# A new order of work in the attention part of a fused attention and feed-forward kernel: sync queue, weight operations, score thirds and key products

## The chip, the core and the metric

The kernel runs on one core of a Trainium2 chip. Its engines are TensorE (PE, with its weight loads shown as PEld), VectorE (DVE), ScalarE (ACT), GpSimd (POOL) and SyncE (SP), which here only issues DMAs. Each engine works through its own list of instructions in order, and they meet at semaphores. The metric is the device time of one execution in microseconds.

## What is computed

The first part is attention over 8 batches, 12 heads, 448 positions and a head size of 64, with scores capped by a tanh. Its output, put back to 8 x 448 x 768, goes through a feed-forward layer that mixes each position with the one before it.

```
scores = cap * tanh(scale * q @ k.T / cap)
attn = exp(scores - max) / (sum + 1e-9)
x = attn @ v                                   # -> (8, 448, 768)
xk = mu_k * x + (1 - mu_k) * x_prev            # x_prev: one position earlier
xr = mu_r * x + (1 - mu_r) * x_prev
k = relu(xk @ w_k)                             # 768 -> 1024
out = sigmoid(xr @ w_r) * ((k * k) @ w_v)
```

The weights come as 64-bit floats and are turned into 32-bit ones by the kernel itself.

## The kernel before

**Steps.** The 96 heads are taken as 48 pairs. The first part of the kernel is a loop of 54 steps (`NSTEP`), one for each pair and six that drain it. What one step emits is written out as a list of words; `step` reads it from left to right, and so each engine's order is the order of the words. There are four lists: `START_EVEN` and `START_ODD` for the steps below `SW` (14), `EVEN` and `ODD` for the rest. Step i works on several pairs at once:

- `S0`, `S1`, `S2` (L216): scores of pair i, one third of the keys each, into a PSUM tile `s`, of which there are two, taken in turn. `L` (L227), in even steps, is the leftover 64 keys of pairs i and i+1, done in quadrants of the array. For pairs below 14 (`RAW`) the scores multiply the loaded floats themselves; later pairs use a high and a low part that POOL makes two steps ahead (`qk_high`, `qk_low`).
- `tanh`, `exp` (L237, L243) on ACT; `red` (L273) on DVE sums the exponentials.
- `V` (L252): values of pair i-1, into a PSUM tile `pv`, of which there are two. `VL` (L262) adds the leftover keys of pairs i-2 and i-1, in quadrants too.
- `gather` (L282): four small DMAs that bring the sums of pair i-1 together, `recip` (L286, DVE) inverts them, `rec_store` (L294) and `rec_load` (L297) send the result through DRAM and back as a broadcast.
- `norm` (L303, DVE), `mix_old` (L306, ACT), `mix_new` (L316, DVE), `x_high`, `x_low` (L322, L325, POOL), `x_store` (L331): pair i-2 is normalised, mixed and split. `mix_old` overwrites the `pv` tile, and `mix_new` is the last to read it, so it is `mix_new` of pair i-2 that frees the tile for `V` two pairs on.
- `K` (L342): some of the 1152 matmuls of `xk @ w_k`, 18 to a PSUM tile `kps`, of which there are two. `KE` and `KO` tell how many each of the four `K` words of an even and an odd step makes: 28 in an even step, 20 in an odd one, from step 7 on (`KFIRST`). `relu` (L360, ACT) and `k_store` (L367, a DMA issued by ACT) take out every tile finished so far.
- `weight_load` (L374) brings one of 44 weight pieces; `more` brings a second one in the steps that `MORE` names. `weight_abs` (L392, ACT) and five operations `f` (L415 to L423, DVE; `weight_rest` does all that are left) convert it, `weight_sum` (L428, POOL) and, for `w_k`, `weight_low` (L441, DVE) finish it, `weight_store` (L447) sends the pieces of `w_r` and `w_v` to DRAM.

**Queues.** All loads and stores but `k_store` are issued by SP, in the order of the words, so an issue that waits for a semaphore holds up every later one. `gather` waits for the last `red` of the step before, `rec_store` for `recip`, `rec_load` for the landing of `rec_store`.

**The second part** (L660 on) runs 28 chunks of 128 positions through `w_r` and `w_v`. Nothing in it is changed.

Of the kernel before, what the change touches and what calls it, by code (L numbers as in the profile page):

```python
# [38 lines left out]
QA = QM + KL  # L39
NSTEP = NPAIR + 6  # L40
RAW = 14
SW = 14
MORE = (1, 7, 8, 9, 10)
KFIRST = 28
KE, KO, KT = (7, 7, 7, 7), (5, 5, 5, 5), 8
HALF = (slice(0, 64), slice(64, 128))
NB = 2 * S // 32

# [2 lines left out]

START_EVEN = """gather weight_load load_v load_vl more load_qk weight_low S0 S1 K V VL L weight_rest f norm f tanh0 exp0
qk_high weight_sum tanh1 exp1 relu k_store f recip red0 qk_low tanhL K S2 mix_old mix_new x_high x_low red1
tanh2 relu expL redL exp2 k_store K K red2 f f weight_abs relu k_store rec_store rec_load x_store
weight_store"""
START_ODD = """gather more load_qk load_v weight_load f f f S0 S1 V S2 f f weight_low K tanh0 relu exp0 norm red0
weight_rest weight_sum tanh1 recip rec_store qk_high tanh2 mix_old mix_new x_high qk_low x_low k_store exp2 K
red2 relu exp1 red1 k_store K K relu weight_abs k_store weight_store x_store rec_load"""  # L60
EVEN = """weight_load gather load_vl load_v load_qk weight_rest weight_low f S0 S1 V VL L S2 f f tanh1 tanh0 exp1 exp0
qk_high weight_sum norm recip x_store more K qk_low tanhL relu mix_old red1 mix_new x_high x_low k_store K
expL relu tanh2 redL f f red0 exp2 red2 k_store K K relu k_store weight_abs rec_store rec_load weight_store"""
ODD = """gather more weight_store load_v weight_load f weight_rest S0 S1 V S2 weight_low f K relu tanh0 k_store exp0
red0 qk_high weight_sum tanh1 f norm f recip load_qk rec_store K exp1 red1 f tanh2 mix_old mix_new x_high
qk_low x_low exp2 relu k_store weight_abs K K relu k_store red2 rec_load x_store"""


def f(ap):
# [3 lines left out]
class Body:  # L73
# [446 lines left out]
    def step(self, i):  # L520
# [9 lines left out]
        nk = 0  # L530
        for op in ((START_EVEN if even else START_ODD) if i < SW else EVEN if even else ODD).split():
            g = ()
# [12 lines left out]
            elif op == "more":  # L545
                for _ in range(MORE.count(i)):
                    self.weight_load()
# [170 lines left out]
```

## Time and profile before

| | |
|---|---|
| median of the runs | 983.07 us |
| lowest of the runs | 980.41 us |
| the profiled execution | 981.96 us |
| its span, first to last instruction | 979.8 us |
| PE busy in the span | 937.7 us |
| DVE busy | 652.7 us |
| ACT busy | 478.1 us |
| POOL busy | 255.4 us |

The busy time of PE is that of overlapping matmuls with modelled ends, so an engine shown busy can still lose some tenths of a microsecond at each wait. In the rows below, an arrow `<-` behind a time in brackets names what ended an engine's idle time, by tile and line; SPq and ACTq are DMA issues. Where an engine waits for several semaphores, the one that came last is named.

### The profile page before, as it was taken

What the parts mean: (1) busy time and instruction counts of PE and PEld (TensorE: products, weight loads), DVE (VectorE), ACT (ScalarE), POOL (GpSimd) and SP (SyncE); (2) the same over time, 40 slices, a digit from 0 to 9 for tenths busy, and PEclk for the clock granted to TensorE, in tenths of its full rate; (3) what the DMA queues carried; (4) which work ended last, traced back from release to release, by engine and by line L of the source; (5) the groups of instructions that cost most, each with busy time, mean ns of one, the idle gap of its engine ahead of it and who ended that gap; (6) DMA issues with size and microseconds to landing.
All of it is one profiled execution on the core that took longest, in us unless ns stands there. A gap on an engine that the chain in (4) does not pass through costs nothing.

```text
span 979.8 us, 14498 instructions
## 1 busy us (share of the span) xinstructions
PE 937.7 (96%) x5244; PEld 737.8 (75%) x5244; DVE 652.7 (67%) x1126; ACT 478.1 (49%) x578; POOL 255.4 (26%) x289
## 2 busy tenths in 40 slices
PE   5878999999999999999999999999999999999997
PEld 1225556656666656666667889999999999999997
DVE  5889998798878888885554685554564464464460
ACT  6877787768777877777774112221221221221220
POOL 1434445455555555545431210000000000000000
PEclk9789999999999999999999999999999999999999
DMA  5455555665656656665534843332332332233220
GB/s 163 144 171 179 192 180 188 178 213 182 202 173 193 207 177 188 193 191 157 167 109 131 265 141 88 105 108 67 96 109 71 91 108 78 84 108 86 78 70 35
DMA packets 124704, 138.85 MB, mean 142 GB/s; under 512 B 19664, under 2 KB 109776, under 8 KB 124624
## 3 DMA queue, kind: packets, MB, share of 16 engines
q1 hardware_dynamic: 115408, 123.16, 41.6%
q10 hardware_dynamic: 9216, 14.68, 4.0%
q8 instruction: 43, 0.70, 0.3%
q14 instruction: 37, 0.30, 0.1%
HBM read 92.64 MB, written 42.40 MB: 138 GB/s over the span
## 4 chain that ended last, share of the span: by engine, by line
PE 52%; DVE 21%; DMA 17%; SPq 5%; ACT 3%; issue 2%; POOL 0%; DVEq 0%; ACTq 0%; POOLq 0%
PE pvv L500 23%; PE pr L500 17%; DVE r L275 7%; DMA sq<-r 6%; PE kps L356 5%; SPq L284 4%; PE pv L259 3%; DMA rec_d<-rs 3%; DVE wt L415 3%; DMA r<-rec_d 2%; PE s L224 2%; DVE sr L288 2%; DVE wa L417 2%; DVE xk L319 1%; DMA w<-wr 1%
## 5 line engine op out<-in xcount | busy, mean ns | idle before, releaser
L91 ACT CAST xh<-t 128x768 fp32r<-128x768 f32 x27 | 22.6, 838 | 308.7 <-DVE t L483 308.7
L275 DVE TRANSPOSE_TENSOR_REDUCE r<-p 128x28 f32<-128x896 f32 x144 | 153.4, 1076 | 13.4 <-ACT p L250 13.1
L240 ACT ACTIVATE p<-s,scl_t 128x896 f32<-128x896 f32 x144 | 141.1, 995 | 17.6 <-PE s L224 14.6
L250 ACT ACTIVATE p<-p,cap_t 128x896 f32<-128x896 f32 x144 | 147.3, 1039 | 2.4
L515 DVE TENSOR_TENSOR o<-pvv,rsg 128x768 f32<-128x768 f32 (+1 forms) x29 | 27.0, 930 | 181.2 <-PE pvv L500 180.3
L356 PE MATMUL kps<-xkh,wkh 128*128 128x448 f32 x384 | 143.8, 374 | 2.8 <-ACT ko L363 2.6
L259 PE MATMUL pv<-p,rv 128*64 128x448 f32 x576 | 127.2, 579 | 20.0 <-DMA rv<-v 13.2
L356 PE MATMUL kps<-xkl,wkh 128*128 128x448 f32 x384 | 142.7, 371 | 0.0
L356 PE MATMUL kps<-xkh,wkl 128*128 128x448 f32 x384 | 140.6, 366 | 0.0
L500 PE MATMUL pvv<-wvh,kl 128*128 128x384 f32 x448 | 115.0, 334 | 0.0
L500 PE MATMUL pvv<-wvh,kh 128*128 128x384 f32 x448 | 114.9, 334 | 0.0
L500 PE MATMUL pvv<-wvl,kh 128*128 128x384 f32 x448 | 114.9, 334 | 0.0
L259 PEld LDWEIGHTS pv<-p,rv 128*64 128x64 f32 x576 | 39.5, 143 | 87.6 <-issue 53.7
L356 PEld LDWEIGHTS kps<-xkh,wkh 128*128 128x128 f32 x384 | 72.1, 188 | 20.7 <-issue 9.9
L500 PE MATMUL pr<-wrh,xh 128*128 128x384 f32 x336 | 85.5, 335 | 1.1 <-ACT xh L91 0.8
L500 PE MATMUL pr<-wrh,xl 128*128 128x384 f32 x336 | 85.5, 335 | 1.0 <-DVE xl L491 1.0
L500 PE MATMUL pr<-wrl,xh 128*128 128x384 f32 x336 | 85.2, 334 | 0.0
L356 PEld LDWEIGHTS kps<-xkl,wkh 128*128 128x128 f32 x384 | 72.1, 188 | 13.4 <-issue 7.8
L500 PEld LDWEIGHTS pvv<-wvh,kh 128*128 128x128 f32 x448 | 81.0, 188 | 0.0
L500 PEld LDWEIGHTS pvv<-wvh,kl 128*128 128x128 f32 x448 | 81.0, 188 | 0.0
L500 PEld LDWEIGHTS pvv<-wvl,kh 128*128 128x128 f32 x448 | 81.0, 188 | 0.0
L356 PEld LDWEIGHTS kps<-xkh,wkl 128*128 128x128 f32 x384 | 72.2, 188 | 7.3 <-issue 2.0
(75 smaller groups left out, 1435.7 us busy)
## 6 DMA issues: line engine op xcount, KB each, us to landing
rqk<-qk SPq DMA_DIRECT2D x47, 448.0 KB
k_d<-ko ACTq DMA_DIRECT2D x64, 224.0 KB
kr<-k_d SPq DMA_DIRECT2D x28, 512.0 KB
x_d<-x SPq DMA_DIRECT2D x48, 224.5 KB
r<-rec_d SPq DMA_DIRECT2D x96, 112.0 KB
out<-o SPq DMA_DIRECT2D x27, 384.0 KB
xc<-x_d SPq DMA_DIRECT2D x24, 387.0 KB
rv<-v SPq DMA_DIRECT2D x48, 192.0 KB
```

What stands on the lines that cost most here:

```text
L91: self.nc.scalar.copy(out, x)
L224: nc.tensor.matmul(s[:, h, 0:S], qk[a][p, k], qk[b][p, 0:S], start=(n == 0), stop=(n == len(terms) - 1))
L240: self.nc.scalar.activation(p32, self.S.pop((i, g))[:, :, 0:S], AF.Tanh, scale=self.scl_t)
L250: self.nc.scalar.activation(p32, p32, AF.Exp, scale=1.0 if self.maxima else self.cap_t)
L259: nc.tensor.matmul(pv[p, 0:S], v[:, g, h, :], ph[:, h, :], start=(g == 0), stop=False)
L275: self.nc.vector.tensor_reduce(out=r1[:, :, 3 if g == "L" else g], in_=self.P32[i, g].rearrange("p h (b k) -> p (h b) k", k=32), axis=mybi ...
L284: self.nc.sync.dma_start(self.sq[i % 2][:, q], self.r1[i % 2][32 * q:32 * q + 32])
L288: nc.vector.tensor_reduce(out=t[:, 0:NB], in_=self.sq[i % 2].rearrange("l q x g -> l x q g"), axis=mybir.AxisListType.XY, op=ALU.add)
L356: nc.tensor.matmul(self.kps[fc][:, 0:S], w, m[:, dc, :], start=first, stop=last)
L415: nc.vector.tensor_scalar(t, sq, W_TINY, W_HUGE, op0=ALU.max, op1=ALU.min)
L500: self.nc.tensor.matmul(ps[:, m, 0:HN], a[:, c, :], w[:, c, m * HN:m * HN + HN], start=(c == 0 and part == 0), stop=(c == n - 1 and part = ...
L515: nc.vector.tensor_mul(o[:, q], pv[:, q, 0:HN], rs[:, q])
```

## The change

The four lists are written anew, and five constants with them. No operation on data is added or taken out.

- The sync queue: in `EVEN` the gather comes ahead of the weight load; in `START_ODD` the load of queries and keys three pairs ahead (`load_qk`) comes ahead of the gather; in the other lists `load_qk` moves from ahead of `rec_store` to behind it, in `ODD` behind `weight_store` as well. `rec_store` now stands in the middle of `EVEN`, and `rec_load` ends the queue's list or stands next to its end.
- In `ODD` and `START_ODD`, `mix_new` comes earlier: in `ODD` it follows `recip` with one sum of the step ahead of it instead of two, in `START_ODD` it stands ahead of `recip`. In `START_ODD` `mix_old` stands ahead of `tanh2`.
- `S2` comes ahead of `VL` and `L` in `EVEN`; `S1` comes ahead of `S0` in the odd lists.
- The five weight operations of `EVEN` lie around `red0` instead of ahead of all sums.
- `K` is cut as 9, 6, 5, 8 and 4, 4, 3, 9; `START_EVEN` begins with a `K`; `relu` and `k_store` follow the second `K` of `EVEN` ahead of `tanh2`.
- `MORE` has step 5 in place of step 8, and the start lists end at step 12.

```diff
-SW = 14
-MORE = (1, 7, 8, 9, 10)
+SW = 12
+MORE = (1, 5, 7, 9, 10)
 KFIRST = 28
-KE, KO, KT = (7, 7, 7, 7), (5, 5, 5, 5), 8
+KE = (9, 6, 5, 8)
+KO = (4, 4, 3, 9)
+KT = 8
...
-START_EVEN = """gather weight_load load_v load_vl more load_qk weight_low S0 S1 K V VL L weight_rest f norm f tanh0 exp0
-qk_high weight_sum tanh1 exp1 relu k_store f recip red0 qk_low tanhL K S2 mix_old mix_new x_high x_low red1
-tanh2 relu expL redL exp2 k_store K K red2 f f weight_abs relu k_store rec_store rec_load x_store
-weight_store"""
-START_ODD = """gather more load_qk load_v weight_load f f f S0 S1 V S2 f f weight_low K tanh0 relu exp0 norm red0
-weight_rest weight_sum tanh1 recip rec_store qk_high tanh2 mix_old mix_new x_high qk_low x_low k_store exp2 K
-red2 relu exp1 red1 k_store K K relu weight_abs k_store weight_store x_store rec_load"""
-EVEN = """weight_load gather load_vl load_v load_qk weight_rest weight_low f S0 S1 V VL L S2 f f tanh1 tanh0 exp1 exp0
-qk_high weight_sum norm recip x_store more K qk_low tanhL relu mix_old red1 mix_new x_high x_low k_store K
-expL relu tanh2 redL f f red0 exp2 red2 k_store K K relu k_store weight_abs rec_store rec_load weight_store"""
-ODD = """gather more weight_store load_v weight_load f weight_rest S0 S1 V S2 weight_low f K relu tanh0 k_store exp0
-red0 qk_high weight_sum tanh1 f norm f recip load_qk rec_store K exp1 red1 f tanh2 mix_old mix_new x_high
-qk_low x_low exp2 relu k_store weight_abs K K relu k_store red2 rec_load x_store"""
+START_EVEN = """gather more weight_load load_vl load_v f weight_low weight_rest K S0 S1 V VL L norm tanh0 exp0 tanh1
+weight_sum qk_high exp1 relu k_store f f recip red0 tanhL K relu S2 mix_old mix_new x_high x_low qk_low red1
+tanh2 expL redL exp2 red2 f f weight_abs k_store K K relu k_store rec_store load_qk x_store weight_store
+rec_load"""
+START_ODD = """load_qk gather more load_v weight_load f f f f f weight_low S1 S0 V K S2 tanh0 relu exp0 norm red0
+weight_rest weight_sum tanh1 mix_old mix_new recip qk_high x_high x_low tanh2 qk_low k_store exp2 K red2 relu
+exp1 red1 k_store K K relu k_store weight_abs rec_store x_store rec_load weight_store"""
+EVEN = """gather load_vl weight_load load_v S0 S1 V S2 VL L f weight_low f tanh0 exp0 red0 f f weight_rest f weight_sum
+tanh1 exp1 norm recip rec_store load_qk K qk_high qk_low tanhL mix_old mix_new red1 x_high x_low relu k_store
+K relu k_store K K tanh2 expL redL exp2 red2 relu weight_abs k_store weight_store more x_store rec_load"""
+ODD = """gather weight_load load_v weight_low f S1 S0 V S2 weight_rest tanh1 exp1 red1 tanh0 exp0 weight_sum norm
+recip more x_store rec_store K mix_old f mix_new f f x_high qk_high qk_low red0 tanh2 exp2 red2 f x_low
+weight_abs relu k_store K relu k_store K K relu k_store weight_store load_qk rec_load"""
```

## Rows read from the trace of the kernel before

**Rows 1.** The table by stretch: the window in us, its length, then for each engine its busy time with the number of instructions, the granted TensorE clock as a share of full speed, the DMA engines' busy share and GB/s.

```profile
18.00:92.00 74.00, 57.59 (x262) 21.77 (x262) 63.74 (x111) 54.33 (x64) 26.05 (x37) 0.86 0.50 160
92.00:160.00 68.00, 65.81 (x338) 37.57 (x337) 62.00 (x104) 52.01 (x67) 31.30 (x40) 1.00 0.61 198
160.00:540.00 380.00, 370.62 (x2138) 246.14 (x2136) 289.83 (x420) 281.55 (x343) 186.81 (x196) 1.00 0.56 178
540.00:980.00 440.00, 432.13 (x2466) 428.47 (x2464) 228.50 (x470) 76.70 (x91) 9.35 (x9) 1.00 0.34 99
```

**Rows 2.** The waits of PE by what ended them: us in total, how often, the longest. The first row is of the stretch 92 to 160 us, the other three of 160 to 540 us.

```profile
PE kps L356 <- ACT ko L363: 1.0, 1, 1.0
...
PE pv L259 <- DVE xk L319: 6.8, 7, 2.1
PE kps L356 <- ACT ko L363: 1.6, 2, 1.0
...
PEld pv L259 <- DVE xk L319: 10.8, 11, 2.5
```

**Rows 3.** The timeline of one even step: start in us, length, engine, line and operation, tiles, count, and in brackets the idle time ahead of it with what ended it. L224 is `S0`, `S2` and the next step's first scores, L275 a `red`, L319 `mix_new`, L259 `V`, L268 `VL`, L356 `K`.

```profile
328.33 0.48 PE L224 MATMUL s<-qkh 64*128 64x448 f32 x2
...
329.04 1.06 DVE L275 TRANSPOSE_TENSOR_REDUCE r<-p 128x28 f32<-128x896 f32 x1
...
330.03 0.62 DVE L319 SCALAR_TENSOR_TENSOR xk<-x,mu_k,pv 128x448 f32<-128x448 f32 x1
...
330.71 2.48 PE L259 MATMUL pv<-p,rv 128*64 128x448 f32 x12 [0.88 <-DVE xk L319]
...
333.12 0.98 PE L268 MATMUL pv<-p_left,rvl 64*64 64x448 f32 x8
...
334.78 0.47 PE L224 MATMUL s<-qkh 64*128 64x448 f32 x2
...
335.59 0.47 PE L356 MATMUL kps<-xkl,wkh 128*128 128x448 f32 x1
...
341.46 0.47 PE L224 MATMUL s<-qkh 64*128 64x448 f32 x2
```

**Rows 4.** The same timeline, SP's issues and the operation that waits for them: `rec_store`, `rec_load` (two DMAs), `gather` (four), and on DVE the first operation of `recip`.

```profile
329.13 0.33 SPq L295 DMA_DIRECT2D rec_d<-rs  x1
...
332.53 1.12 SPq L300 DMA_DIRECT2D r<-rec_d  x2
...
334.85 2.44 SPq L284 DMA_DIRECT2D sq<-r  x4
...
339.25 0.61 DVE L288 TENSOR_REDUCE sr<-sq 32x28 f32<-32x448 f32 x1 [1.91 <-DMA sq<-r]
```

**Rows 5.** ACT's instructions at the end of that step: a `relu`, the `k_store` behind it, a `tanh`; and the row of ACT's waits in 160 to 540 us of an `exp` that stands behind such a `k_store`.

```profile
341.57 0.55 ACT L363 ACTIVATE ko<-kps 128x448 f32<-128x448 f32 x1 [0.18 <-PE kps L356]
...
343.58 0.35 ACTq L369 DMA_DIRECT2D k_d<-ko  x1
...
344.49 1.00 ACT L240 ACTIVATE p<-s,scl_t 128x896 f32<-128x896 f32 x1
...
ACT p_left L250 <- DMA sq<-r: 7.2, 4, 2.3
```

**Rows 6.** The waits of DVE (three rows) and of ACT (one) in 18 to 92 us.

```profile
DVE x L304 <- PE pv L268: 3.6, 3, 1.6
DVE sr L288 <- DMA sq<-r: 2.4, 4, 0.7
DVE wt L415 <- ACT wsq L395: 1.8, 2, 1.4
...
ACT wsq L395 <- DMA w<-wk: 14.3, 6, 4.0
```

**Rows 7.** The timeline around the passage from step 5 to step 6: SP's `load_qk` (448 KB) and `weight_load` (384 KB; between them stands `load_v`, 192 KB), PE's `V`, ACT's `weight_abs`, DVE's first weight operation and `norm`.

```profile
58.87 0.57 SPq L164 DMA_DIRECT2D rqk<-qk  x1
...
60.02 0.38 SPq L383 DMA_DIRECT2D w<-wk  x1
...
62.78 4.75 PE L259 MATMUL pv<-p,rv 128*64 128x448 f32 x12 [3.61 <-DMA rv<-v]
...
65.14 0.55 ACT L395 ACTIVATE wsq<-w 128x384 f32<-128x384 f32 x1 [4.01 <-DMA w<-wk]
...
65.72 0.36 DVE L415 TENSOR_SCALAR wt<-wsq 128x384 f32<-128x384 f32 x1 [1.35 <-ACT wsq L395]
...
69.08 0.63 DVE L304 TENSOR_TENSOR x<-pv,r 128x448 f32<-128x448 f32 x1 [1.03 <-PE pv L268]
```

**Rows 8.** Groups of DVE's instructions in 18 to 92 us that one weight piece costs: count, busy time, mean ns of one.

```profile
L423 DVE SCALAR_TENSOR_TENSOR wsq<-w,wt 128x384 f32<-128x384 uint32 x9 | 5.0, 559 | 0.3
L419 DVE SCALAR_TENSOR_TENSOR wa<-w,wa 128x384 uint32<-128x384 uint32 x9 | 5.0, 559 | 0.3
L443 DVE TENSOR_TENSOR wkl<-wsq,wkh 128x384 fp32r<-128x384 f32 x8 | 5.0, 631 | 0.0
L415 DVE TENSOR_SCALAR wt<-wsq 128x384 f32<-128x384 f32 x9 | 4.4, 488 | 1.9 <-ACT wsq L395 1.8
...
L417 DVE TENSOR_SCALAR wa<-wt 128x384 uint32<-128x384 uint32 x9 | 3.6, 404 | 0.3
L421 DVE TENSOR_SCALAR wt<-wa 128x384 uint32<-128x384 uint32 x9 | 3.2, 359 | 0.3
```

## The prediction

> **What bounds the kernel now.** I read the table by stretch first [rows 1]. From 540 us on, PE is idle for 440.00 - 432.13 = 7.9 us of 440 in the second part, which the change leaves alone. From 160 to 540 us it is idle for 380.00 - 370.62 = 9.4 us, from 92 to 160 us for 2.2 us: there the steps run at the pace of PE, and no order of the others' work can give back more than these. Only in 18 to 92 us is PE idle for long (16.4 of 74 us), at a granted clock of 0.86; but there DVE is busy for 63.74 us, so that stretch can shrink by at most 74.00 - 63.74 = 10.3 us. So the reader is to see a small prize before any edit is looked at: 9.4 + 2.2 + 10.3 = 21.9 us of 982.
>
> Next the waits that make up PE's idle time [rows 2]. In 160 to 540 us, 6.8 us stand ahead of `V`, waiting for `mix_new`, and 1.6 us ahead of `K`, waiting for a `relu`; in 92 to 160 us another 1.0 us for a `relu`. For the opening I read the waits of DVE and ACT [rows 6] and the passage between two steps [rows 7]: ACT stands still for 14.3 us in `weight_abs`, because the weights land late, and DVE for 3.6, 2.4 and 1.8 us behind `VL`, the gather and `weight_abs`.
>
> **Part by part: the wait for `mix_new`.** In the even step shown [rows 3], the scores run from 328.33 to 329.83, `V` could start there, and starts at 330.71, 0.06 us after `mix_new` ends at 330.65. This is `mix_new` of the odd step before, late because two sums (1.06 us each) and `recip` stand ahead of it. In the new `ODD` one sum stands ahead, in the new `START_ODD` not even `recip`. So `mix_new` ends about one sum earlier, and a wait of up to 1.06 us goes. The seven waits have a mean of 0.97 us and a longest of 2.1; of that longest one about 1 us stays. That gives 6.8 - 1.0 = 5.8, taken as 6.0 us because the weight loads' row of the same wait shows 10.8 us [rows 2], part of which is lost inside what counts as busy. The ends are 0 and 10.8 us. What is late next: `exp2` of the pair before, or the values' load; neither shows as a wait of `V` in this stretch.
>
> **The cut of `K` and the place of `relu`.** A `kps` tile is 18 matmuls, and the order in which the first two tiles of a batch are finished leaves three matmuls (3 x 0.21 = 0.6 us, with 5.87 us for 28 matmuls in rows 3) between the end of one tile and the start of the next that needs its buffer. A `relu` takes 0.55 us [rows 5]. In the old `EVEN`, that `relu` stands behind an `exp`; in the new one it follows the second `K`, in which the tile ends (20 + 9 + 6 = 35 covers matmul 33). The 1.6 + 1.0 us fall to about 0.1 us each; I take 2.0 us off. The ends are 0 and 2.6.
>
> **The third scores.** `S2` moves from behind `L` to ahead of `VL`: the same matmuls, and five changes of tile shape in the step before and after. I cost it at nothing; what covers it is that `tanh0` (1.0 us) ends under `V` (330.71 to 333.12, 2.4 us), which frees the score tile for `S2`.
>
> **The sync queue.** In the step shown [rows 4], `rec_store` went out at 329.13, `rec_load` waited for it until 332.53, `x_store` and the weight load came next, and so the gather began only at 334.85 and DVE waited 1.91 us for it at 339.25. With `rec_store` in mid-step, and only `rec_load` ahead of the gather, the queue is about 1 us ahead; DVE waits less. In 160 to 540 us that is worth nothing beyond the 6.0 us above, since DVE is busy for 290 of 380 us and PE sets the pace. `load_qk` goes out later in most lists, at about `recip` instead of the head: in `EVEN` some 8 us. Its first reader, POOL, comes a step later, and the scores two steps after that; I cost it at nothing, and at 0.5 us a step if that cover were gone. Stores last (`x_store`, `weight_store`) delay nobody in this part, as what they write is read only at the passage to the second part.
>
> **The opening.** Between steps 5 and 6 [rows 7] the weight load is issued at 60.02 and ends ACT's wait at 65.14, 5.1 us later, behind 448 KB of `load_qk` and 192 KB of values. With `load_qk` ahead of the gather, those 448 KB move while the gather is issued (2.44 us in rows 4): 448/1024 of 5.1, 2.2 us, come off the landing in each odd step. But the stretch is DVE's: of its waits [rows 6] the 2.4 us for the gather lose about 1.9 (`mix_new`, 0.62 us, now stands ahead of `recip` in three odd steps), and of the 3.6 + 1.8 us I take half, 2.7, because `V` there waits for the values' load too, which stays behind the gather. Against it stands `MORE`: one piece comes to step 5 from step 8. A piece costs DVE 0.49 + 0.40 + 0.56 + 0.36 + 0.56 + 0.63 = 3.0 us [rows 8]; the step that gets it has 1.35 + 1.03 us of idle DVE [rows 7], so it costs 0.6 us; where it left, PE is full and nothing comes back. Opening: -1.9 - 2.7 + 0.6 = -4.0 us, with ends of -10.3 (all of DVE's idle time) and +3.0 (a whole piece, no gain).
>
> A rule of the Trainium skill weighs in here: "DMA: Bandwidth & Descriptors", section "Anatomy of one DMA", gives about 2 us plus the bytes at 436 GB/s for a transfer. By it the 448 KB would take 1.05 us and the weights alone 2.9 us, against 5.1 us in rows 7; the gain of an odd step would be 1.05 us instead of 2.2, which moves nothing in the sum, as DVE bounds it, but speaks for the smaller half.
>
> **The sum.** -4.0 (opening) - 2.0 (`relu`) - 6.0 (`mix_new`) = -12.0 us. The profiled execution took 981.96 us, so 970.0 us; it lay 1.1 us under the median of 983.07 us, and I leave it there.
>
> **Rivals.** *A, the opening gives everything.* ACT's 14.3 us and the slow clock of `V` (4.75 us at 62.78 against 2.48 at 330.71) are one chain; if it breaks, all 10.3 us of DVE's idle time go: 981.96 - 10.3 - 8.0 - 1.4 (what is left of PE's 9.4) = 962.3. Against it: values and weights still stand behind the gather, and `mix_old` now delays `tanh2` and `exp1` by 1 us.
>
> *B, nothing moves.* `V` waits for something else once `mix_new` is early, and the extra weight piece eats the opening: 981.96 - 2.0 (`relu`) = 980.0. For it: nearly all of PE's time is work.
>
> *C, slower: a `k_store` holds up `tanh2`.* In the new `EVEN`, `k_store` stands ahead of `tanh2`, and the next step's first score needs the tile that `tanh2` reads. In rows 5 a `relu` ended at 342.12 and its `k_store` left only at 343.58; an `exp` behind such a store waited four times for the gather's landing, 1.8 us in the mean. By rows 3 the new even step is 1.50 (scores) + 2.41 (`V`) + 0.81 (`S2`) + 1.66 (`VL`, `L`) + 5.87 (`K`) = 12.25 us, and the second `K` ends at 6.38 + 15 x 0.21 = 9.53; `relu` 0.55, `k_store` 0.4 and `tanh2` 1.0 make 11.5. So 0.75 us are spare. From a hold-up of 0.75 us on, PE pays; at 1.5 us in each of 17 even steps the gain of 12 us is gone; at 1.8 us it costs 1.05 x 17 = 18 us: 988. Against it: the gather now leaves earlier and should have landed long before.
>
> *D, `load_qk` comes too late.* If POOL waits for it, at 0.5 us in 34 steps: 987. By the issue at `recip` (339.25 + 1.2) and 5.1 us of landing it is there some 5 us into the next step, where POOL needs it at about 6; a wait of POOL reaches PE only through later pairs. "DMA: Bandwidth & Descriptors", section "Rules for kernel authors", says to issue a DMA early and wait late, and by that rule this edit goes the wrong way.
>
> **How the numbers follow.** Forecast 0.53 (its own range 964 to 977), A 0.15, B 0.20, C 0.10, D 0.02. The range for eight in ten takes the forecast, B and half of A: 962 to 984. Two per cent, about what a measurement of this kernel can tell from no change, is 19.6 us: faster than 962.4 needs A in full, 0.10; slower than 1001.6 needs C at the longest hold-up of 2.3 us ((2.3 - 0.75) x 17 = 26, to 996) and the opening's loss as well, 0.04; the rest, 0.86, is within.
>
> **What would show it.** Right: in 160 to 540 us PE's idle time falls from 9.4 to about 2 us and the wait of `V` for `mix_new` is gone; `K` waits for `relu` under 0.3 us each; in the opening ACT's wait for weights falls from 14.3 us to 8 or less, and scores of step 8 start about 4 us earlier. Wrong: a new wait of scores for `tanh2` in each odd step (C), of `V` for values or `exp2` (B), of POOL for the queries' load (D), or an opening of under 66 us between the same steps (A).

## The result and the profile after

| | before | after |
|---|---|---|
| median of the runs | 982.27 us | 963.93 us |
| lowest of the runs | 980.41 us | 963.39 us |
| the profiled execution | 981.96 us | 964.25 us |
| its span | 979.8 us | 962.4 us |

The ratio of the times is 0.982, with a 95% interval of 0.9801 to 0.984. One of the four runs of the kernel before, of 2274.65 us, is left out of the ratio but stands in the median of the table; without it the median is 981.47 us, and the change made the kernel 17.5 us faster. The kernel before was run 39 times more beside the experiments, with a median of 979.2 us (974.5 to 987.4). So some 3 of the 17.5 us may be chance in its first runs, the traced one (981.96 us) among them, and 15 us is the careful figure. The forecast was 970.0 us, its own range ended at 964, the range for eight in ten at 962.

The table by stretch of the kernel after, with the columns of [rows 1]; the last window ends with the span:

```profile
18.00:92.00 74.00, 57.27 (x270) 22.36 (x269) 70.00 (x122) 57.39 (x68) 28.45 (x40) 0.91 0.55 168
92.00:160.00 68.00, 67.98 (x351) 40.35 (x350) 61.02 (x101) 53.26 (x67) 33.34 (x39) 1.00 0.66 201
160.00:540.00 380.00, 379.89 (x2191) 255.70 (x2190) 287.97 (x427) 283.70 (x343) 186.16 (x196) 1.00 0.61 187
540.00:962.00 422.00, 416.12 (x2391) 414.60 (x2389) 218.32 (x458) 74.03 (x86) 5.03 (x4) 1.00 0.32 92
```

From 160 to 540 us PE is idle for 380.00 - 379.89 = 0.1 us, where it was 9.4 us [rows 1], and from 92 to 160 us for 0.02 instead of 2.2 us. No wait of a PE matmul is listed in either stretch, so all of [rows 2] is gone. In 18 to 92 us PE's idle time is what it was (16.7 us against 16.4), while DVE's busy time rose from 63.74 to 70.00 us and the granted clock from 0.86 to 0.91: the opening does more work in the same window, and still has PE waiting.

To see where in time the 17.5 us of span went, compare when `V` of the same pair starts in both traces. `V` of pair 7 starts 1.5 us earlier, of pair 14 4.6, of pair 38 15.0, the first matmul of the second part 16.0, the end 17.5. So 10.4 us come between pairs 14 and 38, the steady part under `EVEN` and `ODD`, 4.6 us before it, and 1.5 us in the second part, where nothing was changed. The early figures scatter: in three kernels below with the same start lists (a_mix_late, a_s2_back, a_rec_adjacent), pair 7 starts 3.5, 2.1 and 4.0 us earlier than before, pair 10 4.2, 3.8 and 4.3 (after: 3.2), pair 14 5.6, 5.3 and 5.7. The trace of the kernel before is itself late there: b_mix_early, b_gather_first, b_queue and b_fill, which leave its start lists as they are, reach pair 14 1.0 to 2.4 us earlier than it. In the mean of five traces with the old start lists and five with the new ones (after, these three and a_k_even), the opening gives 4.2 us by pair 14.

What changed in an even step of that part: the timeline of the kernel after, SP's issues (`rec_store` L297, `weight_store` L452, `load_qk` L166, `rec_load` L302, `gather` L286), PE's `V`, and DVE's first operation of `recip` and `mix_new`.

```profile
314.77 0.34 SPq L297 DMA_DIRECT2D rec_d<-rs  x1
...
315.20 0.32 SPq L452 DMA_DIRECT2D w_d<-wsq  x1
...
315.61 0.38 SPq L166 DMA_DIRECT2D rqk<-qk  x1
...
317.18 1.12 SPq L302 DMA_DIRECT2D r<-rec_d  x2
...
318.39 2.45 SPq L286 DMA_DIRECT2D sq<-r  x4
...
319.30 2.48 PE L261 MATMUL pv<-p,rv 128*64 128x448 f32 x12
...
324.07 0.60 DVE L290 TENSOR_REDUCE sr<-sq 32x28 f32<-32x448 f32 x1
...
325.99 0.68 DVE L321 SCALAR_TENSOR_TENSOR xk<-x,mu_k,pv 128x448 f32<-128x448 f32 x1 [0.74 <-ACT pv L316]
```

Here the gather leaves 0.91 us ahead of `V`; in [rows 3, 4] it left 334.85 - 330.71 = 4.14 us behind it. `recip` starts 4.77 us after `V` and waits for nothing; there it started 8.54 us after `V`, 1.91 us of it standing still.

The waits of SP and of DVE in 160 to 540 us, first before, then after, show the same for the whole part:

```profile
SPq L300 <- DMA rec_d<-rs: 88.7, 35, 4.2
...
DVE sr L288 <- DMA sq<-r: 38.3, 26, 2.7
```

```profile
SPq L302 <- DMA rec_d<-rs: 27.3, 26, 3.1
...
DVE sr L290 <- DMA sq<-r: 3.9, 8, 0.8
```

Before, SP stood for 88.7 of 380 us at `rec_load`, until the `rec_store` just ahead of it had landed, with the gather and all loads behind it. After, 27.3 us are left, and `recip` waits for the gather 3.9 instead of 38.3 us.

The waits of 18 to 92 us after (PE, ACT and DVE), and below them two of PE before, which [rows 6] does not have:

```profile
PE s L226 <- ACT p L242: 11.6, 8, 3.9
...
ACT pv L316 <- DVE x L306: 10.3, 5, 3.8
...
PE pv L261 <- DMA rv<-v: 3.3, 2, 2.4
...
ACT wsq L397 <- DMA w<-wk: 3.0, 3, 1.4
...
DVE sr L290 <- DMA sq<-r: 0.8, 2, 0.6
DVE x L306 <- DMA sq<-r: 0.7, 1, 0.7
```

```profile
PE pv L259 <- DMA rv<-v: 12.9, 4, 4.5
PE s L224 <- ACT p L240: 2.9, 5, 0.8
```

ACT's wait for weights fell from 14.3 to 3.0 us and PE's for the values from 12.9 to 3.3 us, but `mix_old` now waits 10.3 us for `norm`, and PE's scores wait 11.6 instead of 2.9 us for the `tanh` that stands behind it on ACT. One wait took the place of another.

### The profile page after: what moved, and what is told of

Its sections match the earlier page's. It is cut to its first block, busy times and chain, and to the rows that moved or that the text cites. A ratio compares the mean times of both kernels' runs of the same rounds, so it can differ in the third digit from the quotient of the medians.

```text
span 962.4 us, 14423 instructions
## 1 busy us (share of the span) xinstructions
PE 932.7 (97%) x5244; PEld 736.9 (77%) x5244; DVE 646.0 (67%) x1126; ACT 482.0 (50%) x578; POOL 254.9 (26%) x289
## 4 chain that ended last, share of the span: by engine, by line
PE 87%; DVE 6%; DMA 4%; ACT 1%; SPq 1%; issue 1%; POOL 1%; DVEq 0%; POOLq 0%
PE pvv L502 23%; PE kps L358 22%; PE pr L502 17%; PE pv L261 11%; PE s L226 10%; PE pv L270 2%; PE s L236 2%; DVE r L277 1%; DMA wst<-w_d 1%; DMA r<-rec_d 1%; SPq L286 1%; DMA sq<-r 1%; DMA xc<-x_d 1%; DVE wrl L575 0%; DVE t L485 0%
## 5 line engine op out<-in xcount | busy, mean ns | idle before, releaser
L277 DVE TRANSPOSE_TENSOR_REDUCE r<-p 128x28 f32<-128x896 f32 x144 | 156.5, 1095 | 26.0 <-ACT p L252 25.1
L242 ACT ACTIVATE p<-s,scl_t 128x896 f32<-128x896 f32 x144 | 143.7, 998 | 37.9 <-PE s L226 30.1
L252 ACT ACTIVATE p<-p,cap_t 128x896 f32<-128x896 f32 x144 | 149.5, 1041 | 3.7
L261 PE MATMUL pv<-p,rv 128*64 128x448 f32 x576 | 122.5, 562 | 3.3 <-DMA rv<-v 3.3
L261 PEld LDWEIGHTS pv<-p,rv 128*64 128x64 f32 x576 | 38.3, 140 | 70.8 <-issue 51.5
L432 POOL TENSOR_TENSOR wsq<-wa,wsq 128x384 f32<-128x384 f32 x44 | 45.1, 1025 | 128.1 <-DVE wsq L425 121.9
```

What stands on the lines that cost most here:

```text
L242: self.nc.scalar.activation(p32, self.S.pop((i, g))[:, :, 0:S], AF.Tanh, scale=self.scl_t)
L252: self.nc.scalar.activation(p32, p32, AF.Exp, scale=1.0 if self.maxima else self.cap_t)
L261: nc.tensor.matmul(pv[p, 0:S], v[:, g, h, :], ph[:, h, :], start=(g == 0), stop=False)
L277: self.nc.vector.tensor_reduce(out=r1[:, :, 3 if g == "L" else g], in_=self.P32[i, g].rearrange("p h (b k) -> p (h b) k", k=32), axis=mybi ...
L432: {"p": self.nc.gpsimd, "v": self.nc.vector}[e].tensor_add(sq, f(a), sq)
```

## The experiments

Two theories were set against each other for the steady part. P, the prediction's: `mix_new` was late in DVE's list, and its new place freed `pv` for `V`. R, the round trip: `rec_load` right behind `rec_store` held SP for the landing, so gather, `recip` and everything behind `recip` on DVE were late, `mix_new` among them. The first three expectations call R by the name Q; in later ones R stands against G, by which only the place of the gather in `EVEN` counts. The ranges for kernels built on the one before were set from the 982 us of its traced run, 3 us more than it then took beside them. Each kernel is compared with runs of the kernel before on the same chip. Line numbers of kernels built on the one after are higher by two.

For the reading, four numbers were worked out from each trace. For every pair from 14 to 37 I took the start of its gather and of the first operation of its `recip`, each less the start of the last `V` begun before that `recip`, and the time from the issue of `rec_store` to that of `rec_load`. The means stand as odd steps / even steps, 12 each. The last column is how much earlier (-) or later (+) than before pair 38 is reached, less the same for pair 14, in us, by one trace of each kernel. The trace of before has a stretch at a lower clock between these pairs (below, in the section on the prediction), which is worth 1.6 us in this column.

| kernel | gather after `V` | `recip` after `V` | `rec_load` after `rec_store` | pair 14 to 38 |
|---|---|---|---|---|
| before | 2.39 / 4.11 | 6.34 / 8.63 | 3.66 / 2.97 | 0 |
| b_mix_early | 2.53 / 4.27 | 6.52 / 8.65 | 3.34 / 2.97 | -5.4 |
| b_gather_first | 3.28 / 3.81 | 7.36 / 7.57 | 3.61 / 5.05 | +11.7 |
| b_queue | -1.04 / -0.84 | 3.50 / 4.18 | 2.09 / 1.84 | -11.1 |
| b_fill | -0.95 / -0.51 | 3.62 / 5.01 | 1.59 / 1.81 | -11.1 |
| after | -0.08 / 0.40 | 3.83 / 5.12 | 2.93 / 2.13 | -10.4 |
| a_mix_late | -0.08 / -0.02 | 3.80 / 5.05 | 2.62 / 1.96 | -10.4 |
| a_rec_adjacent | 1.76 / 3.62 | 7.26 / 8.26 | 1.91 / 1.92 | -0.4 |

### `mix_new`'s place or the sync queue

**b_mix_early**: before, with `mix_old mix_new` of `ODD` moved ahead of a sum, a weight operation and `tanh2`.

```diff
-... K exp1 red1 f tanh2 mix_old mix_new x_high
+... K exp1 mix_old mix_new red1 f tanh2 x_high
```

> The kernel before with one edit in ODD: mix_old and mix_new stand behind exp1, ahead of red1, instead of behind red1 and tanh2. Theory P (place): V waited because one sum too many stood ahead of mix_new; without it the 6.8 to 10.8 us of waits between 160 and 540 us go, and the kernel takes 973 to 976 us. Theory Q (queue): mix_new was late because recip waited for a late gather; then this edit changes little, 980 to 982 us.

Measured: 975.87 us against 978.92, ratio 0.9965 (0.9936 to 0.9993), 3 us. The time lies in P's range, which was set 3 us too high. The place is worth something alone: in the trace PE's idle time between 160 and 540 us falls from 9.4 to 4.4 us. In time it is less than the 6.0 of the forecast and a quarter of what the queue gives (b_queue). Its profiled execution was its fastest, so the -5.4 of the table is a favourable case.

**a_mix_late**: after, with `mix_old mix_new` of `ODD` put back behind `red0` and `tanh2`.

```diff
-... K mix_old f mix_new f f x_high qk_high qk_low red0 tanh2 exp2
+... K f f f qk_high qk_low red0 tanh2 mix_old mix_new x_high exp2
```

> The changed kernel with one edit in ODD: mix_old behind tanh2 and mix_new behind red0, as late as in the kernel before. Theory P: V of the even steps waits for mix_new again, 970 to 973 us. Theory Q: the queue's order is what counts, 963 to 966 us.

Measured: 964.3 us, ratio 0.9852 (0.9819 to 0.9885), PE busy for 379.89 of the 380 us as in after. With the new queue the place of `mix_new` is worth nothing that can be measured.

**b_queue**: before, with only SP's words of `EVEN` and `ODD` at the places that they have after. Every word of the other engines stays.

```diff
 EVEN
-weight_load gather load_vl load_v load_qk ... recip x_store more K ... rec_store rec_load weight_store
+gather load_vl weight_load load_v ... recip rec_store load_qk K ... weight_store more x_store rec_load
 ODD
-gather more weight_store load_v weight_load ... recip load_qk rec_store K ... rec_load x_store
+gather weight_load load_v ... recip more x_store rec_store K ... weight_store load_qk rec_load
```

> The kernel before with SP's words of EVEN and ODD alone put where the changed kernel has them (gather first, rec_store in mid-step, load_qk behind it, weight_store, x_store and rec_load last); all other words stay in their order. Theory P: DVE's 33 us of waiting for the gather shrink, but V still waits for mix_new behind two sums; 979 to 983 us. Theory Q: recip and mix_new come earlier, V's waits go; 973 to 976 us.

Measured: 966.73 us, ratio 0.9877 (0.9838 to 0.9915), 12 us of the 15 to 18, and under the range of either theory. The waits of 160 to 540 us of b_queue, of SP and DVE:

```profile
SPq L300 <- DMA rec_d<-rs: 11.6, 18, 1.2
...
DVE sr L288 <- DMA sq<-r: 0.8, 2, 0.6
```

SP's wait falls from 88.7 to 11.6 us, `recip`'s from 38.3 to 0.8, no wait of a PE matmul is listed any more, and so that of `V` for `mix_new` [rows 2] is gone, although `mix_new` was not moved. So the place of `mix_new` is not needed for the steady gain, and with the new queue adds nothing to it (a_mix_late); R stands.

### What it is in the queue

**b_fill**: before, with two words of each list moved. `load_qk` goes from ahead of `rec_store` to behind it, and `rec_load` behind one or two other DMAs. The gather stays where it was.

```diff
 EVEN
-weight_load gather load_vl load_v load_qk ... rec_store rec_load weight_store
+weight_load gather load_vl load_v ... rec_store load_qk weight_store rec_load
 ODD
-... recip load_qk rec_store K ... red2 rec_load x_store
+... recip rec_store K ... red2 load_qk x_store rec_load
```

> The kernel before with issues put between rec_store and rec_load in EVEN and ODD: load_qk (from ahead of rec_store) and weight_store in EVEN, load_qk and x_store in ODD; nothing else moves. Theory R (round trip): rec_load right behind rec_store held SP for the landing (88.7 us of waits between 160 and 540 us) and with it the next gather; filled, that wait falls under 35 us, V's waits for mix_new go and the kernel takes 967 to 971 us. Theory G (gather first): what counts is that nothing stands ahead of the gather in EVEN; then 977 to 982 us here.

Measured: 969.53 us, ratio 0.9888 (0.9843 to 0.9934), 10 us. Two words moved in either list bring nearly the whole steady gain, with the gather where it was, so G falls. Its waits in 160 to 540 us, of SP and DVE:

```profile
SPq L300 <- DMA rec_d<-rs: 4.9, 9, 0.9
...
DVE sr L288 <- DMA sq<-r: 9.0, 15, 1.0
```

**a_rec_adjacent**: after, with `rec_load` right behind `rec_store` in `EVEN` and `ODD`.

```diff
-recip rec_store load_qk K ... x_store rec_load
+recip rec_store rec_load load_qk K ... x_store
-recip more x_store rec_store K ... load_qk rec_load
+recip more x_store rec_store rec_load K ... load_qk
```

> The changed kernel with rec_load right behind rec_store in EVEN and ODD. Theory R: SP stands still for the round trip again, its waits there grow from 27 to over 80 us; the gather is already out by then, so that what is late is the loads and stores behind it, and a part of the gain goes: 966 to 974 us. Theory G: the gather still leads, 963 to 965 us.

Measured: 974.77 us, ratio 0.9946 (0.9921 to 0.9971), 11 us over after and over a_tanh2_first, which ran beside it. That is just over R's range, though SP's wait did not grow to over 80 us, as R had it. Its waits in 160 to 540 us, of SP, DVE and PE:

```profile
SPq L302 <- DMA rec_d<-rs: 45.5, 34, 3.1
...
DVE sr L290 <- DMA sq<-r: 55.8, 30, 3.8
...
PE pv L261 <- DMA rv<-v: 5.2, 7, 1.4
PE pv L261 <- DVE xk L321: 2.6, 3, 0.9
PE kps L358 <- ACT ko L365: 1.8, 4, 0.6
```

This one word's place undoes the steady gain (-0.4 in the table) and brings back the waits of before: `recip` for the gather, `V` for `mix_new` and now for the values too, whose load stands behind the gather, and `K` for `relu`. SP stands at `rec_load` for only 45.5 / 34 = 1.3 us each time, yet `recip` waits 55.8 us: the price is not the wait on SP but what is behind it.

Why so little weighs so much can be read from the same traces. SP's order closes a ring: the gather leads to `recip`, `recip` to `rec_store`, its landing to `rec_load`, and behind `rec_load` on SP stands the next gather. From start to start, in odd / even steps for the same pairs, these four legs take 3.95 / 4.52, 1.28 / 1.22, 3.66 / 2.97 and 2.33 / 2.35 us in before, and 5.50 / 4.64, 1.22 / 1.22, 1.91 / 1.92 and 2.91 / 2.85 us in a_rec_adjacent: 11.1 us a step in both. In after, where PE waits for nothing, a step takes 10.6 us. By these means the ring and not PE sets the pace in the two slower kernels, and what lengthens a leg lengthens the step. In a_rec_adjacent the store lands soon, but the issues that filled its landing now stand behind `rec_load`, and in odd steps the way from the gather to `recip` is longer. In after the fourth leg is 3.81 us in even steps, because the gather waits there for its step's last sum (at 331.62 us for one that ends at 331.59): the ring has time to spare.

**b_gather_first**: before, with only the first two words of `EVEN` swapped.

```diff
-EVEN = """weight_load gather load_vl load_v load_qk ...
+EVEN = """gather weight_load load_vl load_v load_qk ...
```

> The kernel before with one word moved: in EVEN the gather stands ahead of the weight load. Theory R: 0.4 us of issue time a step, while rec_load ahead of it still waits; 979 to 982 us. Theory G: 967 to 972 us.

Measured: 992.49 us, ratio 1.0129 (1.0085 to 1.0173): 13 us slower, which neither theory gave. Its waits in 160 to 540 us, of SP, PE and ACT:

```profile
SPq L300 <- DMA rec_d<-rs: 115.0, 34, 5.2
...
PE pv L259 <- DVE xk L319: 9.7, 11, 2.4
PE s L224 <- ACT p L240: 8.5, 11, 1.5
...
ACT p_left L250 <- DMA w<-wv: 6.7, 2, 3.5
```

Two things got worse. `rec_store` lands later (`rec_load` 5.05 us after it in even steps, 2.97 before), which fits the 384 KB of weights that now go out closer ahead of it. And scores wait 8.5 us for a `tanh`, for which they waited 0.5 us before. Its timeline shows one such wait: SP's weight load, then ACT's `k_store` (ACTq), the `exp` and the `tanh` behind it, and PE's scores.

```profile
320.65 0.53 SPq L387 DMA_DIRECT2D w<-wv  x1
...
324.19 0.33 ACTq L369 DMA_DIRECT2D k_d<-ko  x1
...
324.56 1.04 ACT L250 ACTIVATE p_left<-p_left,cap_t 128x896 f32<-128x896 f32 x1 [3.54 <-DMA w<-wv]
...
325.51 0.99 ACT L240 ACTIVATE p<-s,scl_t 128x896 f32<-128x896 f32 x1
...
326.55 0.48 PE L224 MATMUL s<-qkh 64*128 64x448 f32 x2 [1.54 <-ACT p L240]
```

The `k_store` stood at its issue until SP's weight load had landed, and ACT behind it, for 3.54 us. Counted from ACT's timeline in 160 to 540 us (time from the end of the instruction ahead to the store's issue, where over 0.25 us), such hold-ups are 11 with 14.5 us in before, 17 with 26.7 us here, 2 with 0.8 us in a_rec_adjacent, and none in after, b_queue and b_fill. As a_rec_adjacent loses the steady gain all the same, these hold-ups are not what the gain of b_queue and b_fill hangs on.

### The cut of `K` and the third scores

**a_k_even**: after with the old cut of `K`.

```diff
-KE = (9, 6, 5, 8)
-KO = (4, 4, 3, 9)
+KE = (7, 7, 7, 7)
+KO = (5, 5, 5, 5)
```

> The changed kernel with K cut as before, 7, 7, 7, 7 and 5, 5, 5, 5. Theory K: the cut carries the 2.0 us that were forecast for the waits behind relu: 965.5 to 967 us, with waits of K for relu near 1 us each. Theory N: relu's place in the list and ACT's free time do it, whatever the cut: 963 to 965 us.

Measured: 964.05 us, ratio 0.9837 (0.9793 to 0.9881); PE busy for 379.89 us, no matmul of `K` waiting for a `relu`. The cut is worth nothing that can be measured.

**a_s2_back**: after with `S2` of `EVEN` behind `VL` and `L` again.

```diff
-... S0 S1 V S2 VL L f ...
+... S0 S1 V VL L S2 f ...
```

> The changed kernel with S2 behind VL and L again in EVEN. As forecast it is worth nothing: 963 to 965 us. Rival: S2 ahead of the quadrants lets tanh2 run earlier and so spares waits of the next scores: 966 us or more here.

Measured: 963.16 us, ratio 0.983 (0.9785 to 0.9876); PE busy for 379.83 us. Worth nothing, as forecast.

### The opening

**b_start**: before with the new `START_EVEN` and `START_ODD` only; `SW`, `MORE` and the rest as before.

> The kernel before with the two start lists of the changed kernel and nothing else (MORE, the end of the start lists at step 14, K and the other two lists as before). If the opening's gain is the lists' own: V of pair 7 about 4.4 us and V of pair 14 about 5 us earlier than before, and after that the waits of the kernel before: 976 to 979 us. If it hangs on the rest: 980 us or more.

Measured: 971.9 us, ratio 0.9918 (0.9886 to 0.9951), 7 us, some 4 us under the range of the expectation. `V` of pair 7 starts 5.8 us earlier, of pair 14 7.5, so the start lists by themselves give at least all that the whole change gives there. In the steady part it keeps before's waits: `rec_load` waits 82.3 us for `rec_store`'s landing, and pair 38 is only 2.0 us further ahead than pair 14, of which 1.6 us are the lower clock in the trace of before.

**a_more_8**: after with the second weight piece in step 8 instead of 5.

```diff
-MORE = (1, 5, 7, 9, 10)
+MORE = (1, 7, 8, 9, 10)
```

> The changed kernel with MORE back at (1, 7, 8, 9, 10): the extra weight piece of step 5 goes to step 8. Theory P1: DVE sets the pace up to step 7, so a piece costs it 3.0 us there in full and nothing later where PE is full: V of pair 7 comes 3 us earlier and the kernel takes 961 us. Theory P2: the steps from 8 to 13 are DVE's too, so that the piece costs the same 3 us wherever it is: V of pair 7 comes 3 us earlier, V of pair 14 does not, and the kernel takes 964 us. As forecast (0.6 us where it went, nothing where it left): 963.5 us.

Measured: 962.79 us, ratio 0.9828 (0.9796 to 0.9861). The time does not decide between the 961, 964 and 963.5 us that were set against each other. `V` of pair 10 starts 5.9 us earlier than before, where after and the three kernels with its start lists have 3.2 to 4.3; at pair 14 it is 5.0, and they have 4.6 to 5.7. So by these traces the piece costs 1.6 to 2.7 us where it goes, and all of it comes back where it left. The same edit on top of a_tanh2_first (a_both, below) still leads by 1.6 us at pair 14, so whether all comes back is not settled. DVE is busy for 67.87 us of 18 to 92.

**a_tanh2_first**: after with `tanh2` of `START_ODD` ahead of `mix_old` again.

```diff
-weight_rest weight_sum tanh1 mix_old mix_new recip qk_high x_high x_low tanh2 qk_low ...
+weight_rest weight_sum tanh1 tanh2 mix_old mix_new recip qk_high x_high x_low qk_low ...
```

> The changed kernel with one edit in START_ODD: tanh2 ahead of mix_old, as in the kernel before. Theory T: in the opening ACT waits 10.3 us in mix_old for norm with tanh2 behind it, and S1 of the next step waits up to 4 us for that tile; with tanh2 first V of steps 4 and 6 comes earlier and the kernel takes 961 to 963 us. Theory D: DVE, busy for 70 of 74 us, is the bound of the opening; 963 to 965 us.

Measured: 963.72 us, ratio 0.9831 (0.9789 to 0.9874); `V` of pair 14 starts 6.4 us earlier than before, 0.6 us ahead of the best of those four. The waits of PE in its 18 to 92 us:

```profile
PE pv L261 <- DMA rv<-v: 8.8, 3, 4.7
PE s L226 <- ACT p L242: 3.8, 7, 0.8
PE pv L261 <- DVE xk L321: 3.0, 1, 3.0
```

The scores' wait falls from 11.6 to 3.8 us (8.8 to 10.3 in the three kernels with the same start lists), and the values' wait takes its place (3.3 to 8.8): PE goes from one late thing to the next.

**a_both**: after with both of these edits.

> The changed kernel with MORE at (1, 7, 8, 9, 10) and tanh2 ahead of mix_old in START_ODD. If the two edits of the opening add up: V of pair 14 about 7 us earlier than in the kernel before (the changed one: 4.6), 961 to 963 us, ahead of both kernels by a little. If DVE's load bounds them together: 963 to 964 us.

Measured: 961.31 us, ratio 0.9804 (0.9766 to 0.9842); `V` of pair 14 starts 8.0 us earlier than before, 2.3 us ahead of the best of those four, and the span is 959.9 us against 962.4. It lies a little ahead of both kernels; its interval overlaps that of after, so that it beats after is likely, not shown. Both edits put back what the change had moved.

## Why the prediction was right in its range and wrong in its cause

**The bound held for PE's idle time, not for the time.** The forecast gave 9.4 us as all that was to be had in 160 to 540 us [rows 1] and 2.2 us in 92 to 160, and PE's idle time fell by 9.3 and 2.2. But between pairs 14 and 38 the change won 10.4 us, where PE had been idle for 8.5. The trace of before shows most of the rest at its longest wait of `V`; the lines are the first operation of `recip`, `mix_new` and `V`.

```profile
195.71 0.61 DVE L288 TENSOR_REDUCE sr<-sq 32x28 f32<-32x448 f32 x1 [1.86 <-DMA sq<-r]
...
197.83 0.63 DVE L319 SCALAR_TENSOR_TENSOR xk<-x,mu_k,pv 128x448 f32<-128x448 f32 x1
...
198.52 4.11 PE L259 MATMUL pv<-p,rv 128*64 128x448 f32 x12 [2.11 <-DVE xk L319]
```

Behind this wait the granted clock was 0.50 from 198.4 to 201.8 us, and `V` took 4.11 instead of 2.48 us, 1.6 us more. So a wait can cost more than its idle time, and "no order of the others' work can give back more" went too far. That the time stayed within the range was in part luck: its lower end of 962 us was made for rival A, an opening that gives everything, and what came instead was a gain from the queue, which had been put at nothing.

**The sync queue was the step that failed.** It was put at nothing "beyond the 6.0 us above, since DVE is busy for 290 of 380 us and PE sets the pace", with the queue "about 1 us ahead". It was 2.5 us ahead in odd steps and 3.7 in even ones (gather after `V`, before against after), and alone it gave 12 us (b_queue). The row was there: in [rows 4] SP does nothing from 329.46, the end of `rec_store`'s issue, to 332.53. I read it as a cost of SP, which has time to spare. But SP's list is in order, and behind `rec_load` stood the gather, behind the gather `recip`, behind `recip` on DVE `mix_new`, and behind `mix_new` `V`. And the next `rec_store` waited for that `recip`, so the ring closed, at 11.1 us a step where PE needs 10.6. The share of busy time of DVE said nothing on this; the order of its list did.

**The `mix_new` term (-6.0)** named the right wait and the wrong reason. `mix_new` was late because what stood ahead of it, `recip`, waited for the gather (1.86 of the 2.11 us above), and in part because of the sum ahead of it. Its new place gives 3 us while the queue is late (b_mix_early) and nothing when it is not (a_mix_late), so no share of the measured gain can be put down to it.

**The `relu` and `K` term (-2.0)**: the waits went, but not by the cut (a_k_even). They go in b_queue too, with the old cut, and come back in a_rec_adjacent with the new one. The late `k_store`s ahead of `relu`s on ACT (14.5 us before, none in b_queue) cannot be the whole reason, as a_rec_adjacent has 0.8 us of them and 1.8 us of this wait. What made those `relu`s late stays open.

**The opening (-4.0)** came out at 4.6 us by pair 14 (up to 5.7 in kernels with the same lists), and of these 2.2 are PE's idle time in 92 to 160 us, of which the forecast had counted 1.0, under `relu`. Taken by the mean of five traces each it is 4.2 us, so the size was right, in part by luck, as the working of `MORE` was not: 0.6 us where the piece goes, and "nothing comes back" where it left. The piece costs 1.6 to 2.7 us, nearer to its 3.0 us of DVE's work [rows 8], and comes back in a_more_8, though not in full in a_both. The objection raised against rival A, that `mix_old` now delays `tanh2`, is what happened, at a price under 2 us (a_tanh2_first). "What would show it" asked for scores of step 8 some 4 us earlier; `V` in that step was 1.5 us earlier, and 2.1 to 4.0 in the other kernels.

**Costed at nothing, and rightly:** the third scores (a_s2_back) and a later `load_qk`, for which POOL does not wait in after between 160 and 540 us. In fact `load_qk` behind `rec_store` helps: b_fill moves it so, and the store then lands sooner.

**The rivals.** A gave 962.3 us, nearly the time measured, by another way: DVE's idle time in 18 to 92 us went from 10.3 to 4.0 us, but the steady part gave twice what the opening gave. A time that fits is no evidence for its cause. C, a `k_store` that holds up `tanh2`, does not occur in after; b_gather_first shows that the mechanism is real and what it costs. D did not occur.

**The rule on DMAs.** "DMA: Bandwidth & Descriptors" of the Trainium skill, section "Rules for kernel authors", says that a DMA that reads what an earlier one wrote has to wait for the earlier one's completion before it is issued, and to issue early and wait late. The first half is the wait of `rec_load` here. The second half is said there of overlap with computing; taken for issues too, it gives the place between store and load to other issues, and b_fill agrees, 10 us for two words in either list. The section "Anatomy of one DMA" of the same page of the Trainium skill gives about 2.0 us of fixed cost for a DMA, fitted to DMAs issued by GpSimd, which the prediction did not say; those here are issued by SP, and a_rec_adjacent shows 1.9 us from `rec_store` to `rec_load`. With larger loads just ahead of the store it was 3.0 to 3.7 us (before) and 5.05 (b_gather_first), for which that figure has no term.

**What stays open.** The place of `rec_load` and `load_qk` does three things at once: SP is held less, the store lands sooner, and each later DMA has another DMA eight places ahead of it (last section). a_rec_adjacent has the early landing without the fill and loses the gain, so the landing alone is not it; the other two were not taken apart, and the ring is read from traces and was not tried by itself. Nor were the weight operations of `EVEN` (before, two of the five already stood between `redL` and `red0`, not all ahead of the sums), `S1` ahead of `S0`, and the end of the start lists at step 12.

## What to carry to other kernels

On a queue that issues in order, a load that depends on a store just ahead of it is not priced by its own wait but by what stands behind it: follow the first late issue through each engine's list up to the bound engine, and see whether the way leads back to the queue. Put independent issues between the store and its load, and large loads behind a small store that somebody waits for, not ahead of it. When a wait of the bound engine names an instruction, ask what made that instruction late before moving it.

## What the runs showed of the hardware

The stores that ACT issues can wait for transfers that SP issued. In the records, this program's DMAs take eight completion semaphores in turn (101 to 106, 108 and 110), SP's and ACT's together, and an issue waits on the number that it takes. The `k_store` at 324.19 us of b_gather_first waits on 104, last taken by the weight load at 320.65 us, and leaves once that has landed. So a word moved on SP changes for which transfer a store on ACT waits: in before, four `k_store`s ahead of this `exp` were held by a gather piece (14 KB, [rows 5]); after the swap of two words four were held by a 384 KB load, and in all 17 hold-ups took 26.7 us instead of 11 with 14.5. "Rules for kernel authors" in the same page of the Trainium skill says to give a DMA a semaphore of its own; no run here did so.

The granted clock fell to 0.5 in the steady part of two traces, for 3.4 us each time, right behind the longest wait of `V` for `mix_new`: 2.11 us in before and 2.44 us in b_gather_first, where `V` then took 4.04 us. In b_queue, b_fill and after, which have no such wait, it stayed at 1.0 from 160 to 540 us.
